# Five chunks of up to 128 keys, a block-diagonal P, a 64-byte pad tile, and low weight words read as unsigned integers

## The chip, the cores and the metric

One core of one Trainium2 chip runs the whole program. The metric is the device time of one execution in microseconds, the median of three executions. One more execution was recorded by the hardware profiler; all rows below come from it.

## The reference, cut to what matters

Three parts run one after another: an attention in two steps, a dense layer, and a layer of eight experts of which each token takes two.

```python
# batch 8, heads 8, seq 576, head_dim 64, 32 rows in p
p_packed = sm_attn(p, k, v)            # 32 query rows against 576 keys
out = sm_attn(q, p_packed, p_packed)   # 576 query rows against the 32 packed rows
x = out as (4608, 512)
h = x @ w_in; g = h - tanh(h); x = g @ w_out      # w_in, w_out are 64-bit floats
...                                               # gate, top 2 of 8 experts, their two matmuls
```

`sm_attn` is softmax attention: scores times 1/8, minus the row's largest, exponential, divided by the row's sum, times the values. The weights `w_in` and `w_out` arrive as 64-bit floating-point numbers, which the kernel turns into 32-bit ones itself.

## The kernel before, in words

The change lies in the first phase (`phase_a`, line 108 of the profile's numbering and on) and in the class `Widen` (line 48 on). The phases after it are the dense layer with the second attention step (`phase_b`, its steps of `g1`, `gate`, `gsplit` and `g2`), and the experts (`PhaseC`).

**Phase A** does the first attention step, `p_packed`, for 16 groups of four heads, and beside it converts weights. It runs 18 steps, n = 0 to 17. Step n computes the scores of group n (`s1`, L175), their largest (`max1`, L180 and L181) and the exponential (`exp1`, L187). For group n-1 it transposes the exponentials on the tensor engine (`t1`, L199), copies them from PSUM to SBUF on ScalarE (`a1t`, L204), multiplies with the values (`pv`, L211), scales and masks on VectorE (`pz2`, L216), transposes (`pt`, L221), copies (`pt_out`, L226) and stores (`pt_store`, L230).

*Scores.* A tile of kT holds 128 partitions: for each of two pairs j of heads, the 64 components of head 0 in partitions 0 to 63 and those of head 1 in partitions 64 to 127, 576 keys and 32 columns of P each. Four matmuls per half c of the keys take 64 rows and 32 columns of the array each and write the 32 rows of their head.

*Values.* The 576 keys are cut in six chunks of 96. So there are six transposes, one copy of 96 x 768, and six times two matmuls of 96 rows and 64 columns, which add up in PSUM. The tile v has 96 partitions of 6 x 256 values, filled by one DMA.

*Weights.* Each step n below 14 also converts two chunks of 128 x 512 weights, c0 = 2n and c1 = 2n+1 (16 of `w_in`, 12 of `w_out`; four more follow in phase B). A chunk arrives as pairs of 32-bit words. `act1` (L69, ScalarE) takes the absolute value of the high word read as a float. `dve` (VectorE) clamps it (L73), shifts it into a 32-bit exponent and mantissa (L75), adds the sign (L76), builds from the low word a float between 1 and 2 by a shift and an or (L78), and cuts the exponent out (L80). `act2` (L84, ScalarE) turns L78's result into the small fraction that the low word stands for. `dve2` (VectorE) multiplies it by the exponent (L88) and adds both parts (L91).

*Order.* The tensor engine, ScalarE and SyncE (which issues the DMAs) work in the order written out by hand in `ORDER` (L103); VectorE's order in this phase is not written by hand. Per step ScalarE runs: `a1t` of n-1, `act1` of c0 (p0), `act2` of c0 (p2), `exp1`, `act1` of c1 (r0), `pt_out` of n-1, `act2` of c1 (r2). The tensor engine runs `t1` of n-1, `s1` of n, `pv` and `pt` of n-1. SyncE issues kT of n+2 (L160), a weight chunk (L144), the store of n-1 (L230), v of n+1 (L166), a weight chunk. There are two buffers of kT and of v, three of the raw weights. In steps 3 to 8 the first piece of the second attention step is put in between (L299 to L335).

**Phase B** starts with the last four chunks of `w_out` converted the same way, in an order written by hand on VectorE too.

**The pool of the experts' small tables** (`consts`, L1101) lies in SBUF above the tiles that were placed after it: among them the 32-bit weights `WI`, the ring `wt`, the first slot of first-layer expert weights and the experts' inputs.

Of the kernel before, what the change touches and what calls it, by code (L numbers as in the profile page):

```python
# [10 lines left out]
F32 = mybir.dt.float32  # L11
FR = mybir.dt.float32r
I32 = mybir.dt.int32
BF = mybir.dt.bfloat16
AF = mybir.ActivationFunctionType
ALU = mybir.AluOpType
# [5 lines left out]
P = 128  # L22
NB, NH, S, D = 8, 8, 576, 64
# [27 lines left out]
class Widen:  # L51
# [19 lines left out]
    def dve(self):  # L71
        V, c = self.K.nc.vector, self.c
        V.tensor_scalar(c, c, EXP_LO, EXP_HI, op0=ALU.max, op1=ALU.min)  # L73
        self.a = a = self.tile("a", I32)
        V.tensor_scalar(a, c.bitcast(I32), 3, 0x3FFFFFFF, op0=ALU.logical_shift_left, op1=ALU.bitwise_and)  # L75
        V.scalar_tensor_tensor(a, self.hi, _sint(0xC0000000), a, op0=ALU.bitwise_and, op1=ALU.bitwise_or)  # L76
        self.f = self.tile("f", I32)
        V.tensor_scalar(self.f, self.lo, 9, 0x3F800000, op0=ALU.logical_shift_right, op1=ALU.bitwise_or)  # L78
        self.t = self.tile("t", I32)
        V.tensor_scalar(self.t, a, _sint(0xFF800000), None, op0=ALU.bitwise_and)  # L80

    def act2(self):
        u = self.f.bitcast(F32)
        self.K.nc.scalar.activation(u, u, AF.Copy, scale=2.0 ** -20, bias=-(2.0 ** -20))  # L84

    def dve2(self):
        G, u = self.K.nc.vector, self.f.bitcast(F32)
        G.tensor_tensor(u, u, self.t.bitcast(F32), op=ALU.mult)  # L88
        if self.w is None:
            self.w = self.t.bitcast(F32)  # L90
        G.tensor_tensor(self.w, u, self.a.bitcast(F32), op=ALU.add)  # L91
# [12 lines left out]
ORDER = """t1 a1t s1 p0 lk p1 max1 p2 p4 pl r4 rec pv pz2 p3 exp1 pt r0 pto pts qs r1 lv qm qx r2 r3 qa rl""".split()  # L104
ENG = {mybir.EngineType.PE, mybir.EngineType.SP, mybir.EngineType.Activation}
NWA = 12


def phase_a(K, kT, v, w_in, w_out, wide_in, wide_out):
    nc, tc = K.nc, K.tc  # L110
    V, A, SY, PE = nc.vector, nc.scalar, nc.sync, nc.tensor
    K.wof = [None] * 16
    CW = 512
    with ExitStack() as ctx:
# [16 lines left out]
        TT, CV = [{} for _ in range(16)], {}  # L131
# [24 lines left out]
        def load_k(n):  # L156
            b, G = BG[n]
            t = TT[n]
            kp = ld.tile([P, 2, S + 32], F32, tag="kT", name=f"kT{n}")
            SY.dma_start(kp, kT[b, G].rearrange("p (j n) -> p j n", j=2))  # L160
            t["k"], t["p"] = kp[:, :, :S], kp[:, :, S:]

        def load_v(n):
            b, G = BG[n]
            TT[n]["v"] = ld.tile([96, 6, 4 * D], F32, tag="v", name=f"v{n}")
            SY.dma_start(TT[n]["v"], v[b, G].rearrange("p (c n) -> p c n", c=6))  # L166

        def s1(n):
            t = TT[n]
            t["s1"] = psb.tile([P, 2, 512], F32, tag="big", name=f"s1_{n}")  # L170
            for c in range(2):
                for h in range(4):
                    j, r = divmod(h, 2)
                    r = slice(64 * r, 64 * r + 64)
                    PE.matmul(t["s1"][32 * h:32 * h + 32, c, :288], t["p"][r, j, :], t["k"][r, j, c * 288:(c + 1) * 288], start=True, stop=True)  # L175

        def max1(n):
            t = TT[n]
# [16 lines left out]
        def t1(n):  # L195
            t = TT[n]
            t["tp"] = psb.tile([P, 8, P], F32, tag="big", name=f"tp{n}")
            for i in range(6):
                PE.transpose(t["tp"][:96, i, :], t["a1"][:, i * 96:(i + 1) * 96], K.ident)  # L199

        def a1t(n):
            t = TT[n]
            t["a1T"] = wk.tile([96, 6, P], F32, tag="a1T", name=f"a1T_{n}")
            A.activation(t["a1T"], t.pop("tp")[:96, :6, :], AF.Copy)  # L204

        def pv(n):
            t = TT[n]
            t["pv"] = ps.tile([P, 512], F32, tag="ps", name=f"pv{n}")
            for i in range(6):
                for j in range(2):  # L210
                    PE.matmul(t["pv"][64 * j:64 * j + 64, :P], t["a1T"][:, i, 64 * j:64 * j + 64], t["v"][:, i, P * j:P * j + P], start=(i == 0), stop=(i == 5))  # L211

        def pz2(n):
            t = TT[n]
# [645 lines left out]
class PhaseC:  # L860
# [240 lines left out]
    def consts(self):  # L1101
        K, V, mp, G = self.K, self.K.nc.vector, self.mp, self.K.nc.gpsimd
        K.sel = mp.tile([P, 4, 4, 32], F32, name="sel")
        for b in range(4):
            for q in range(4):
                G.tensor_copy(K.sel[:, b, q], K.ident[:, 32 * b:32 * b + 32])

        def halves(p, n, pat, cm, name):
            f, i, j = mp.tile([p, n], F32, name=f"half{name}"), mp.tile([p, n], I32, tag=f"t0{name}", name=f"hi{name}"), mp.tile([p, n], I32, tag=f"t1{name}", name=f"hj{name}")
            o = mp.tile([p, n], F32, name=f"odd{name}")  # L1110
            G.iota(f, pattern=pat, base=0, channel_multiplier=cm, allow_small_or_imprecise_dtypes=True)
            V.tensor_copy(i, f)
            V.tensor_scalar(j, i, 1, None, op0=ALU.bitwise_and)
            V.tensor_scalar(i, i, 1, None, op0=ALU.logical_shift_right)
            V.tensor_copy(f, i)
            V.tensor_copy(o, j)
            even, place = mp.tile([p, n], F32, name=f"even{name}"), mp.tile([p, n], F32, name=f"place{name}")
            V.scalar_tensor_tensor(place, f, 2.0, o, op0=ALU.mult, op1=ALU.add)
            V.tensor_scalar(even, o, 2.0, -1.0, op0=ALU.mult, op1=ALU.add)
            V.tensor_tensor(f, f, even, op=ALU.mult)  # L1120
            V.tensor_scalar(even, o, -1.0, 1.0, op0=ALU.mult, op1=ALU.add)
            return f, even, place

        K.need = mp.tile([P, NE], F32, name="need")
        G.iota(K.need, pattern=[[1, NE]], base=1 - NEARLY, channel_multiplier=0, allow_small_or_imprecise_dtypes=True)
        V.tensor_scalar(K.need, K.need, 128.0, None, op0=ALU.mult)
        V.memset(K.need[:, :NEARLY], -1e6)
        K.last = mp.tile([P, E], F32, name="last")
        V.tensor_scalar(K.last, K.eio, float(E - 1), None, op0=ALU.is_equal)
        K.early = mp.tile([NE, 3], F32, name="early")  # L1130
        G.iota(K.early[:, 0:1], pattern=[[0, 1]], base=0, channel_multiplier=1, allow_small_or_imprecise_dtypes=True)
        K.needc = mp.tile([NE, 1], F32, name="needc")
        V.tensor_scalar(K.needc, K.early[:, 0:1], 128.0, 128.0 * (1 - NEARLY), op0=ALU.mult, op1=ALU.add)
        V.tensor_scalar(K.early[:, 1:2], K.early[:, 0:1], 36.0 * (E - 1) - NEARLY, None, op0=ALU.add)
        V.tensor_scalar(K.early[:, 2:3], K.early[:, 0:1], float(NEARLY), None, op0=ALU.is_ge)
        V.scalar_tensor_tensor(K.early[:, 0:1], K.early[:, 2:3], float(-NEARLY), K.early[:, 0:1], op0=ALU.mult, op1=ALU.add)

        self.planr = halves(1, NM, [[1, NM]], 0, "r")
        self.planc = halves(NM, 1, [[0, 1]], 1, "c")
# [276 lines left out]
def layout(inputs):  # L1416
    import numpy as np
    c = np.ascontiguousarray
    x = {k: np.asarray(v) for k, v in inputs.items()}
    wide = {k: x[k].dtype.itemsize == 8 for k in ("moe_w_in", "moe_w_out")}  # L1420

    def words(t):
        return t.view(np.int64) if t.dtype.itemsize == 8 else t

    def heads(t):
        t = t.reshape(NB, 2, 2, 2, S, D).transpose(0, 1, 3, 5, 2, 4)
        return c(t).reshape(NB, 2, P, 2 * S)

    pt = x["p"].reshape(NB, 2, 2, 2, 32, D).transpose(0, 1, 3, 5, 2, 4)
    a = {  # L1430
        "qT": heads(x["q"]),
        "kT": np.concatenate([heads(x["k"]).reshape(NB, 2, P, 2, S), pt.reshape(NB, 2, P, 2, 32)], -1).reshape(NB, 2, P, 2 * (S + 32)),
        "v": c(x["v"].reshape(NB, 2, 4, 6, 96, D).transpose(0, 1, 4, 3, 2, 5)).reshape(NB, 2, 96, 6 * 256),
        "w_in": words(c(x["moe_w_in"].reshape(4, P, FF).transpose(1, 0, 2))).reshape(P, 4 * FF),
        "w_out": words(c(x["moe_w_out"].reshape(16, P, DM).transpose(1, 0, 2))).reshape(P, 16 * DM),
        "w_gate": c(x["moe2_w_gate"]),
        "w_noise": c(x["moe2_w_noise"]),
        "noise": c(x["moe2_noise"].reshape(NB, 6, 96, E).transpose(0, 2, 1, 3)).reshape(NB, 96, 6 * E),
        "w1": c(x["moe2_w1"].reshape(E, 4, P, 2, 512).transpose(0, 2, 3, 1, 4)).reshape(E, P, 4 * F2),
        "w2": c(x["moe2_w2"].reshape(E, 4, 8, 32, DM).transpose(0, 1, 3, 2, 4)).reshape(E, P, 8 * DM),  # L1440
    }
    return a, wide
# [17 lines left out]
```

## Time and profile before

| what | value |
|---|---|
| three executions: median, lowest, highest | 1700.99, 1699.13, 1701.72 us |
| the profiled execution: time, span of its instructions | 1702.0, 1700.3 us |
| TensorE, VectorE, ScalarE, GpSimd busy | 95%, 66%, 51%, 34% of the span |
| mean granted TensorE clock | 0.968 of full speed |
| moved by DMA | 293.62 MB, mean 173 GB/s |

The profiled execution took 1702.0 us, 1.0 us above the median of the three. Its span, 1700.3 us, is the time from the first instruction to the last; 1.7 us lie around it. Engines are PE (tensor engine's matmuls), PEld (its weight loads), DVE (VectorE), ACT (ScalarE), POOL (GpSimd) and SP (SyncE). In brackets a row says how long the engine was idle before the instruction and what ended that.

### The profile page before, as it was taken

The page shows a single profiled execution, that of the slowest core. Times are in us where ns is not written, and L with a number is a line of the kernel's source. Part 1 is how long each engine was busy: PE and PEld are TensorE (multiplying, and loading weights), DVE is VectorE, ACT ScalarE, POOL GpSimd, SP SyncE. Part 2 cuts the span into 40 slices and gives each one's busy share as a digit, 9 for nine tenths or more (in the row PEclk, how much of TensorE's full clock was granted, in tenths as well). Part 3 has the DMA queues.
Part 4 walks back from the last instruction along what each step waited for, and adds up shares of the span by engine and source line. Part 5 has one row for each costly group of instructions (what it writes and reads, how often), then busy time and mean ns, then how long its engine had stood idle before and what let it go on. Part 6 is the DMA issues. An engine that isn't in the chain of part 4 may idle for free.

```text
span 1700.3 us, 29332 instructions
## 1 busy us (share of the span) xinstructions
PE 1617.0 (95%) x10031; PEld 1372.1 (81%) x10031; DVE 1127.2 (66%) x2900; ACT 873.9 (51%) x1848; POOL 569.9 (34%) x560
## 2 busy tenths in 40 slices
PE   5667999999999999999999999999999999999996
PEld 3334889898989898989977788888888888888885
DVE  7886867676767677876665476666666566666652
ACT  3444555555555555543457665555555555555552
POOL 0000200021212121131555475554444455544421
PEclk7677999999999999999999999999999999999998
DMA  8784267676777777753188346452543624554262
GB/s 277 230 269 142 72 216 238 219 227 217 229 235 240 242 236 244 228 181 115 36 247 261 117 111 208 143 149 51 160 133 100 196 50 143 149 167 128 49 208 46
DMA packets 145655, 293.62 MB, mean 173 GB/s; under 512 B 19679, under 2 KB 69130, under 8 KB 140380
## 3 DMA queue, kind: packets, MB, share of 16 engines
q1 hardware_dynamic: 121676, 252.17, 44.5%
q0 software_dynamic: 23824, 39.51, 12.8%
q8 instruction: 81, 1.33, 0.3%
q14 instruction: 74, 0.61, 0.1%
HBM read 670.57 MB, written 107.59 MB: 458 GB/s over the span
## 4 chain that ended last, share of the span: by engine, by line
PE 84%; DVE 7%; ACT 4%; DMA 2%; issue 1%; POOL 1%; POOLq 0%; DVEq 0%; ACTq 0%
PE acc L503 23%; PE py L1214 21%; PE ph L1173 21%; PE h L478 12%; ACT ht L1195 2%; PE u L444 2%; PE s L175 1%; PE tp L199 1%; PE pv L211 1%; PE sq L299 1%; PE lg L524 1%; DVE cva L76 0%; DMA kT<-in_kT_dram 0%; DVE hl L1204 0%; DMA cvr<-in_w_out_dram 0%
## 5 line engine op out<-in xcount | busy, mean ns | idle before, releaser
L1195 ACT ACTIVATE ht<-h 32x256 f32<-32x256 f32 x660 | 274.7, 416 | 229.8 <-DVE h L1175 209.9
L1006 POOL DMA_INDIRECT x<-x1d,gidxm x264 | 254.9, 966 | 277.1 <-DVE xt L1016 203.2
L503 PE MATMUL acc<-gh,wol 128*128 128x288 f32 x1024 | 302.2, 295 | 0.3 <-POOL wol L101 0.3
L1173 PE MATMUL ph<-w0s,xh 128*128 128x512 f32 x1200 | 301.8, 393 | 0.0
L503 PE MATMUL acc<-gh,woh 128*128 128x288 f32 x1024 | 301.6, 295 | 0.0
L503 PE MATMUL acc<-gl,woh 128*128 128x288 f32 x1024 | 301.4, 294 | 0.0
L1214 PE MATMUL py<-w1s,hh 128*128 128x512 f32 x1200 | 286.8, 391 | 3.4 <-ACT hh L1199 1.8
L1175 DVE STREAM_TRANSPOSE h<-ph 128x512 f32<-128x512 f32 x150 | 107.3, 715 | 246.6 <-PE ph L1173 240.2
L1214 PEld LDWEIGHTS py<-w1s,hh 128*128 128x128 f32 x1200 | 224.6, 188 | 54.6 <-ACT hh L1199 4.7
L1173 PEld LDWEIGHTS ph<-w0s,xh 128*128 128x128 f32 x1200 | 225.1, 188 | 50.8 <-issue 0.5
L659 POOL DMA_INDIRECT table<-d,qi x96 | 97.3, 1013 | 309.9 <-DVE g L487 207.8
L503 PEld LDWEIGHTS acc<-gh,wol 128*128 128x128 f32 x1024 | 192.6, 188 | 0.6 <-POOL wol L101 0.6
L503 PEld LDWEIGHTS acc<-gh,woh 128*128 128x128 f32 x1024 | 193.0, 189 | 0.0
L503 PEld LDWEIGHTS acc<-gl,woh 128*128 128x128 f32 x1024 | 192.7, 188 | 0.0
L485 ACT ACTIVATE t<-h 128x288 f32<-128x288 f32 x256 | 104.4, 408 | 146.4 <-PE h L478 145.9
L1193 DVE TENSOR_SCALAR ht<-h 32x256 f32<-32x256 f32 x540 | 166.5, 308 | 9.9
L478 PE MATMUL h<-a2h,uh 128*128 128x288 f32 x512 | 159.5, 312 | 3.3 <-DVE g L487 2.4
L1173 PE MATMUL ph<-w0s,xl 128*128 128x512 f32 x600 | 162.6, 393 | 0.0
L97 ACT ACTIVATE gh<-g 128x288 fp32r<-128x288 f32 x256 | 113.2, 442 | 87.2 <-DVE g L487 86.2
L487 DVE TENSOR_TENSOR g<-h,t 128x288 f32<-128x288 f32 x256 | 115.7, 452 | 57.0 <-ACT t L485 56.5
L478 PE MATMUL h<-a2h,ul 128*128 128x288 f32 x512 | 151.7, 296 | 0.2 <-DVE ul L453 0.2
L478 PE MATMUL h<-a2l,uh 128*128 128x288 f32 x512 | 151.4, 296 | 0.0
(257 smaller groups left out, 2400.2 us busy)
## 6 DMA issues: line engine op xcount, KB each, us to landing
w0s<-wsp SPq DMA_DIRECT2D x136, 2048.0 KB
w1s<-wsp SPq DMA_DIRECT2D x136, 2048.0 KB
wsp<-wt SPq DMA_DIRECT2D x128, 512.0 KB
wt<-in_w_dram SPq DMA_DIRECT2D x128, 256.0 KB
kT<-in_kT_dram SPq DMA_DIRECT2D x16, 608.0 KB
out_dram<-zero SPq DMA_DIRECT2D x37, 256.0 KB
v<-in_v_dram SPq DMA_DIRECT2D x16, 576.0 KB
q<-in_qT_dram SPq DMA_DIRECT2D x32, 288.0 KB
```

The costliest lines, as they stand in the source:

```text
L97: nc.scalar.activation(hi, src, AF.Copy)
L478: nc.tensor.matmul(h[:, :TN], u[:, G, fs], x[:, G, :], start=(n == 0), stop=(n == 5))
L485: nc.scalar.activation(t, h[:, :TN], AF.Tanh)
L487: PACE[0] = nc.vector.tensor_tensor(g, h[:, :TN], t, op=ALU.subtract).ins
L503: nc.tensor.matmul(ACC[ch][d][:, :TN], w[:, d * P:(d + 1) * P], x, start=(f == 0 and n == 0), stop=(f == 15 and n == 2))
L659: ins = nc.gpsimd.indirect_dma_start(out=K.table, out_offset=IO(ap=qi[:, i:i + 1], axis=0), in_=d[:, i, :], in_offset=None, oob_is_err=True)
L1006: g = K.nc.gpsimd.indirect_dma_start(out=x[:, b, :], out_offset=None, in_=rows, in_offset=IO(ap=gidx[:, c, b:b + 1], axis=0))
L1173: self.tick(K.nc.tensor.matmul(p, xx[:, d * P:(d + 1) * P], w[:, fc, ws, d, :], start=(n == 0), stop=(n == 11)))
L1175: self.last = V.transpose(h[:, 2 * fc:2 * fc + 2].rearrange("p g n -> p (g n)"), p).ins
L1193: V.tensor_scalar(dst, src, 0.0, None, op0=ALU.max)
L1195: K.nc.scalar.activation(dst, src, AF.Relu)
L1214: self.tick(K.nc.tensor.matmul(p, xx[:, f * P:(f + 1) * P], w[:, f // 4, ws, f % 4, :], start=(n == 0), stop=(n == 23)))
```

## The change: what it does

- The keys are cut in five chunks, four of 128 and one of 64: five transposes for six, five times two matmuls for six times two, on up to 128 rows. The copy `a1t` becomes two, 128 x 512 and 64 x 128. The tile v has 128 partitions of 5 x 256 values and is filled by two DMAs, 512 KB and 64 KB (its bytes stay the same).
- P is laid out block-diagonally: 64 columns for each pair of heads, zero where a head's rows meet the other head's columns. So `s1` takes two matmuls of 128 rows and 64 columns per half c for four of 64 rows and 32 columns. The tile kT grows from 608 to 640 values per partition and pair, from 608 KB to 640 KB.
- `Widen` loses L78. `act2` reads the low words as unsigned integers straight from the raw chunk, times 2 to the power -52, and writes the tile f.
- A tile `pad` of 16 values (64 bytes per partition), which nothing reads or writes, is put into the pool of the experts' tables.

```diff
     def dve(self):
...
-        self.f = self.tile("f", I32)
-        V.tensor_scalar(self.f, self.lo, 9, 0x3F800000, op0=ALU.logical_shift_right, op1=ALU.bitwise_or)
+        self.f = self.tile("f", F32)
...
     def act2(self):
-        u = self.f.bitcast(F32)
-        self.K.nc.scalar.activation(u, u, AF.Copy, scale=2.0 ** -20, bias=-(2.0 ** -20))
+        self.K.nc.scalar.activation(self.f, self.lo.bitcast(U32), AF.Copy, scale=2.0 ** -52)
...
+NK = 5
+KL = S - P * (NK - 1)
+KC = [(i, min(P, S - P * i)) for i in range(NK)]
...
-            kp = ld.tile([P, 2, S + 32], F32, tag="kT", name=f"kT{n}")
+            kp = ld.tile([P, 2, S + 64], F32, tag="kT", name=f"kT{n}")
...
-            TT[n]["v"] = ld.tile([96, 6, 4 * D], F32, tag="v", name=f"v{n}")
-            SY.dma_start(TT[n]["v"], v[b, G].rearrange("p (c n) -> p c n", c=6))
+            TT[n]["v"] = t = ld.tile([P, NK, 4 * D], F32, tag="v", name=f"v{n}")
+            vv = v[b, G].rearrange("p (c n) -> p c n", c=NK)
+            SY.dma_start(t[:, :NK - 1], vv[:, :NK - 1])
+            SY.dma_start(t[:KL, NK - 1], vv[:KL, NK - 1])
...
             for c in range(2):
-                for h in range(4):
-                    j, r = divmod(h, 2)
-                    r = slice(64 * r, 64 * r + 64)
-                    PE.matmul(t["s1"][32 * h:32 * h + 32, c, :288], t["p"][r, j, :], t["k"][r, j, c * 288:(c + 1) * 288], start=True, stop=True)
+                for j in range(2):
+                    PE.matmul(t["s1"][64 * j:64 * j + 64, c, :288], t["p"][:, j, :], t["k"][:, j, c * 288:(c + 1) * 288], start=True, stop=True)
...
-            for i in range(6):
-                PE.transpose(t["tp"][:96, i, :], t["a1"][:, i * 96:(i + 1) * 96], K.ident)
+            for i, m in KC:
+                PE.transpose(t["tp"][:m, i, :], t["a1"][:, i * P:i * P + m], K.ident)
...
-            t["a1T"] = wk.tile([96, 6, P], F32, tag="a1T", name=f"a1T_{n}")
-            A.activation(t["a1T"], t.pop("tp")[:96, :6, :], AF.Copy)
+            t["a1T"] = wk.tile([P, NK, P], F32, tag="a1T", name=f"a1T_{n}")
+            tp = t.pop("tp")
+            A.activation(t["a1T"][:, :NK - 1], tp[:, :NK - 1], AF.Copy)
+            A.activation(t["a1T"][:KL, NK - 1], tp[:KL, NK - 1], AF.Copy)
...
-            for i in range(6):
+            for i, m in KC:
                 for j in range(2):
-                    PE.matmul(t["pv"][64 * j:64 * j + 64, :P], t["a1T"][:, i, 64 * j:64 * j + 64], t["v"][:, i, P * j:P * j + P], start=(i == 0), stop=(i == 5))
+                    PE.matmul(t["pv"][64 * j:64 * j + 64, :P], t["a1T"][:m, i, 64 * j:64 * j + 64], t["v"][:m, i, P * j:P * j + P], start=(i == 0), stop=(i == NK - 1))
...
+        mp.tile([P, 16], F32, name="pad")
```

The host's layout of k, p and v follows these tiles (P with its zeros, v padded to 640 keys in memory).

## Rows read from the trace of the kernel before

**Rows 1.** Busy time by stretch: PE, PEld, DVE, ACT, POOL, then granted clock, DMA share, GB/s.
```profile
12.42:30.45 18.03, 12.18 (x94) 7.44 (x94) 14.45 (x35) 6.97 (x14) 0.00 (x0) 0.75 0.91 288
30.45:84.59 54.14, 32.19 (x253) 19.87 (x255) 46.15 (x107) 22.59 (x44) 2.68 (x2) 0.63 0.73 232
84.59:127.12 42.53, 27.59 (x237) 16.57 (x239) 38.05 (x95) 20.85 (x40) 0.00 (x0) 0.70 0.81 271
127.12:143.32 16.20, 12.09 (x96) 7.57 (x98) 12.00 (x31) 6.11 (x12) 0.00 (x0) 0.61 0.80 236
...
210.00:1700.30 1490.30, 1471.22 (x8887) 1272.02 (x8887) 959.60 (x2511) 777.58 (x1653) 549.39 (x515) 1.00 0.57 169
```

**Rows 2.** Timeline of step 4 and its follower: start, duration, instruction.
```profile
38.86 2.15 PE L175 MATMUL s<-kT 64*32 64x288 f32 x16
...
40.30 0.54 SPq L166 DMA_DIRECT2D v<-in_v_dram  x1
...
41.07 0.76 DVE L180 TENSOR_REDUCE nm<-s 128x1 f32<-128x576 f32 x1 [1.70 <-PE s L175]
...
42.68 0.42 DVE L78 TENSOR_SCALAR cvf<-cvr 128x512 int32<-128x512 int32 x1
...
43.13 0.63 ACT L84 ACTIVATE cvf<-cvf 128x512 f32<-128x512 f32 x1 [5.12 <-DVE cvf L78]
...
43.67 0.79 ACT L204 ACTIVATE a1T<-tp 96x768 f32<-96x768 f32 x1
...
44.51 2.83 PE L211 MATMUL pv<-v,a1T 96*64 96x128 f32 x24 [3.51 <-ACT a1T L204]
...
46.33 0.72 ACT L187 ACTIVATE a<-s,nm 128x576 f32<-128x576 f32 x1
```

**Rows 3.** Who waited for whom, 30.45 to 84.59: total, times, longest.
```profile
ACT cvf L84 <- DVE cvf L78: 28.8, 9, 6.3
...
PE pv L211 <- ACT a1T L204: 10.5, 4, 3.5
DVE nm L180 <- PE s L175: 7.7, 5, 1.7
```

**Rows 4.** The same view, 84.59 to 127.12.
```profile
PE pt L221 <- DVE Pz L216: 13.9, 5, 4.7
...
DVE nm L180 <- PE s L175: 3.1, 2, 1.7
```

**Rows 5.** Groups by line and shape, 84.59 to 127.12: count, busy, mean ns.
```profile
L199 PE MATMUL tp<-ident,a 128*96 128x128 f32 x30 | 7.4, 416 | 1.1 <-ACT a L187 1.1
...
L84 ACT ACTIVATE cvf<-cvf 128x512 f32<-128x512 f32 x10 | 6.3, 631 | 6.9 <-DVE cvf L78 6.8
...
L69 ACT ACTIVATE cvc<-cvr 128x512 f32<-128x512 f32 x9 | 6.0, 665 | 0.7 <-DMA cvr<-in_w_out_dram 0.7
...
L78 DVE TENSOR_SCALAR cvf<-cvr 128x512 int32<-128x512 int32 x10 | 4.2, 417 | 0.0
...
L204 ACT ACTIVATE a1T<-tp 96x768 f32<-96x768 f32 x5 | 4.0, 803 | 1.2 <-PE tp L199 1.2
...
L226 ACT ACTIVATE PT<-pt 128x128 f32<-128x128 f32 x5 | 1.3, 269 | 0.6 <-ACT cvc L69 0.6
```

**Rows 6.** VectorE's timeline: an L78 in a busy stretch, and the next instruction.
```profile
94.69 0.42 DVE L78 TENSOR_SCALAR cvf<-cvr 128x512 int32<-128x512 int32 x1
95.02 0.42 DVE L80 TENSOR_SCALAR cvt<-cva 128x512 int32<-128x512 int32 x1
```

**Rows 7.** Busy time in a stretch in which the DMA engines are full.
```profile
110.00:115.00 5.00, 2.09 (x32) 1.29 (x24) 4.29 (x9) 0.90 (x2) 0.00 (x0) 0.84 1.01 336
```

**Rows 8.** Timeline of VectorE and of ScalarE at the last chunk, in phase B.
```profile
201.77 0.42 DVE L78 TENSOR_SCALAR cvf_b<-wor 128x512 int32<-128x512 int32 x1
...
202.23 0.63 ACT L84 ACTIVATE cvf_b<-cvf_b 128x512 f32<-128x512 f32 x1 [2.88 <-DVE cvf_b L78]
```

**Rows 9.** The page's costliest groups: one of phase B's matmuls.
```profile
L503 PE MATMUL acc<-gh,wol 128*128 128x288 f32 x1024 | 302.2, 295 | 0.3 <-POOL wol L101 0.3
```

More of the change, by code (lines that the diff above doesn't have):

```diff
@@ L13 @@
 I32 = mybir.dt.int32
+U32 = mybir.dt.uint32
 BF = mybir.dt.bfloat16
@@ L82, in act2 @@
     def act2(self):
-        u = self.f.bitcast(F32)
-        self.K.nc.scalar.activation(u, u, AF.Copy, scale=2.0 ** -20, bias=-(2.0 ** -20))
+        self.K.nc.scalar.activation(self.f, self.lo.bitcast(U32), AF.Copy, scale=2.0 ** -52)
     def dve2(self):
-        G, u = self.K.nc.vector, self.f.bitcast(F32)
+        G, u = self.K.nc.vector, self.f
         G.tensor_tensor(u, u, self.t.bitcast(F32), op=ALU.mult)
@@ L1427, in heads @@
         return c(t).reshape(NB, 2, P, 2 * S)
-    pt = x["p"].reshape(NB, 2, 2, 2, 32, D).transpose(0, 1, 3, 5, 2, 4)
+    p = x["p"].reshape(NB, 2, 2, 2, 32, D).transpose(0, 1, 3, 5, 2, 4)
+    pt = np.zeros((NB, 2, 2, D, 2, 2, 32), p.dtype)
+    for r in range(2):
+        pt[:, :, r, :, :, r] = p[:, :, r]
+    vp = np.zeros((NB, 2, 4, NK * P, D), x["v"].dtype)
+    vp[:, :, :, :S] = x["v"].reshape(NB, 2, 4, S, D)
     a = {
         "qT": heads(x["q"]),
-        "kT": np.concatenate([heads(x["k"]).reshape(NB, 2, P, 2, S), pt.reshape(NB, 2, P, 2, 32)], -1).reshape(NB, 2, P, 2 * (S + 32)),
-        "v": c(x["v"].reshape(NB, 2, 4, 6, 96, D).transpose(0, 1, 4, 3, 2, 5)).reshape(NB, 2, 96, 6 * 256),
+        "kT": np.concatenate([heads(x["k"]).reshape(NB, 2, P, 2, S), pt.reshape(NB, 2, P, 2, 64)], -1).reshape(NB, 2, P, 2 * (S + 64)),
+        "v": c(vp.reshape(NB, 2, 4, NK, P, D).transpose(0, 1, 4, 3, 2, 5)).reshape(NB, 2, P, NK * 256),
         "w_in": words(c(x["moe_w_in"].reshape(4, P, FF).transpose(1, 0, 2))).reshape(P, 4 * FF),
```

## The prediction

> **What bounds the kernel now.** First the busy time by stretch [rows 1]. From 210 us to the end the tensor engine is busy for 1471.22 of 1490.30 us at full clock, and the change adds and removes no instruction there. So what the first 210 us give up, the whole gives up. The four stretches above it are cut where the scores `s1` of steps 1, 3, 8, 13 and 15 are done; they hold 2, 5, 5 and 2 steps of 9.0, 10.8, 8.5 and 8.1 us. The tensor engine is busy for 65% or less of the two middle ones, at clocks of 0.63 and 0.70. VectorE is busy for 46.15 of 54.14 us and for 38.05 of 42.53 us. The DMA engines are at 0.91 in the first stretch, 0.73 and 0.81 in the next two.
>
> Then one step in order of time [rows 2]. The transposes of group 3 are done when `s1` starts at 38.86. Yet their copy L204 runs at 43.67, because ScalarE works in order and stands before L84 (the `act2` of the chunk before) for 5.12 us, until VectorE has run L78 at 42.68. So `pv` starts at 44.51, after 3.51 us of idle tensor engine, and `exp1` (L187) comes at 46.33, long after the reduction at 41.07. VectorE in turn idles 1.70 us for the scores. Over the five steps of this stretch [rows 3] ScalarE waits 28.8 us for L78, `pv` 10.5 us for the copy and VectorE 7.7 us for scores. In the five steps after it [rows 4] the loop is another one: the tensor engine waits 13.9 us for VectorE's Pz, and VectorE only 3.1 us for scores. There VectorE's own work is the pace.
>
> **The change part by part.** *L78 goes.* A mean instruction takes 0.417 us [rows 5], but in a busy stretch the next one starts 0.33 us after it [rows 6], so 0.33 us is what VectorE gets back: 28 x 0.33 = 9.2 us in phase A, 4 x 0.33 = 1.3 us in phase B.
>
> *The wait of `act2` goes.* It needs only the raw chunk now, which `act1` before it has read already. So the copy L204 follows the transposes, during `s1`, and `pv` follows `s1`. Late next in these steps is VectorE's work.
>
> *`act2` reads words with a step of two, as integers.* No row has ScalarE read integers. Below, 631 ns as now [rows 5]; the nearest row is L69, which reads the other word of each pair with the same step, 665 ns [rows 5]; above, I allow twice that. I take 665: 28 x 0.03 = 1 us of ScalarE, which is busy for 20.85 of 42.53 us [rows 1]; cost 0. Without that cover it is 1 us, at the upper end 28 x 0.7 = 19 us of ScalarE's time, still inside its idle share. The raw buffer is now held until `act2`; the load that waits for it needs the chunk three before, which ScalarE has passed by then: 0.
>
> *`pv` and `t1`.* Twelve matmuls take 2.83 us [rows 2], so ten take 2.36: 0.47 us less at the lower clock. Six transposes take 7.4 / 5 = 1.48 us [rows 5], five 1.23. Together 0.7 us a step on an engine that waits: nothing in steps 2 to 13, but on the chain in the last two, which have no weights beside them: I take 1.0 us there.
>
> *`s1`.* Eight matmuls of 288 columns run four beside each other, 2.15 us [rows 2]. Four matmuls would take the same if they run in pairs, and about twice that one by one. `pv` already runs pairs of 64 columns on the same rows: 0.236 us for a pair of 128 columns, which for 288 gives 0.53 us, and four of those (two halves of keys, two records a matmul) are 2.1 us. I take 0; up to 2 us a step otherwise, most of it in the tensor engine's 2.8 us of wait a step [rows 4].
>
> *`a1t` in two.* 631 + 269 ns (L84's shape, L226's) against 803 [rows 5]: 0.1 us more on ScalarE. It may also gain, as `pv` could start after the first piece: 0, bounds -0.1 and +0.2 us a step.
>
> *v in two DMAs, kT larger.* SyncE issues one more DMA a step, 0.54 us by the row of L166 [rows 2]. Behind it stands one weight chunk, which is read a step later: 0; at most 0.5 us a step without that cover. Per step 2.36 MB move for 2.33. At the 336 GB/s of a full stretch [rows 7] a step needs 7.0 us, 0.1 more. I take 0.2 us in all, at the start, where the first kT is waited for. The Trainium skill (SBUF — State Buffer, "Door 1: The DMA port swizzle") speaks against the split: it asks for 128 partitions and one DMA, since 64 partitions reach half of the ports. By its 196 GB/s for 64 partitions, an estimate, the 64 KB would cost 0.14 us more a step, 2 us in all if the transfers set the pace; no run here shows it, and the sum goes without it.
>
> *The pad* moves the tiles placed after it by 64 bytes. The four buffers of gh in phase B lie 1,152 bytes apart, so at different places within 256 bytes, and their matmuls still take 295 ns in the mean [rows 9]: 0. One per cent of the last stretch would be 15 us either way; I see no sign of it.
>
> **The sum.** VectorE's remaining work plus the idle time that the third stretch shows, 42.53 - 38.05 = 4.5 us in five steps. Second stretch: 46.15 - 3.3 + 4.5 = 47.3 for 54.14, 6.8 us less. Third: 38.05 - 3.3 + 4.5 = 39.2 for 42.53, 3.3 less. The first has its transfers at 0.91: 0.6 less. The last: 1.0 less from VectorE, and 1.0 from the shorter tensor work after the weights are through. Phase B: 1.3 less; ScalarE's 2.88 us wait for L78 there [rows 8] mostly hides under VectorE's queue. With 0.2 for the start: 0.6 + 6.8 + 3.3 + 1.0 + 1.0 + 1.3 - 0.2 = 13.8 us. The profiled 1702.0 becomes 1688.2; the median of the runs stands 1.0 us lower: **1687.2 us**.
>
> **The rivals.** *All waits fall away.* Nothing but VectorE's work and the 7.0 us of transfers a step is left: the second stretch 42.8, the third 35.1, the first 15.6, the last 14.0 us. That is 11.3 + 7.4 + 2.4 + 2.2 less, with 1.0 + 1.3 behind them 25.6 us: 1675.4. For it: the tensor engine has more than 2 us a step to spare [rows 4]. Against: engines working in order never meet so well, and 0.91 for 18 us is the fullest stretch now.
>
> *Transfers set the pace.* If the DMA engines can't be kept fuller than in the third stretch (271 GB/s), a step takes 8.7 us: the third stretch loses 1.0, the first and the last gain nothing, the second still gains 6.8. 6.8 - 1.0 + 1.0 + 1.3 - 0.2 = 7.9 less: 1693.1. For it: two or three buffers a kind, and a store in SyncE's queue that waits for the step's end.
>
> *The time is hidden anyway.* ScalarE stands elsewhere for as long, for a raw chunk or for the reduction before `exp1`, and VectorE waits in place of L78; only 1.0 + 1.3 us are left: 1698.7. Against: the copy L204 has nothing else to wait for in rows 2.
>
> *Slower: VectorE's new order.* Its queue in phase A is not written by hand, and an instruction less may put the reduction of the scores behind weights. The loop from `s1` over reduction, exponential and transposes back to `s1` is 2.15 + 0.9 + 0.9 + 1.2 = 5.2 us. A chunk without L78 is about 2.8 us of VectorE. The loop passes today's 9.4 us a step from 4.2 us of delay on, one and a half chunks; with two it is 10.8, times 13 steps is 18 us more: 1719. Against: the reduction now starts where the scores end, with VectorE waiting for it [rows 2].
>
> **How the numbers follow.** The forecast has 0.52 (1682 to 1692), transfers 0.17, all waits gone 0.16, hidden 0.08, slower 0.07 with what else could go wrong, the pad among it. A measurement of this kernel can tell about 0.2%, 3.4 us, from no change. So faster is 0.52 + 0.17 + 0.16 = 0.85, the same 0.08, slower 0.07. The range leaves out the hidden and the slower case: 1675 to 1697.
>
> **What would show it.** Right: no wait of L84 for VectorE; `pv` starts within 0.3 us of the end of `s1` in steps 2 to 5; five steps from 30 us on take some 47 us, the next five 39; 210 us becomes some 196; the long stretch is unchanged. Wrong: ScalarE's waits move to raw chunks with the DMA share near 0.9 (transfers); L180 starts late after `s1` (order); `s1` takes 4 us (no pairs); a longer last stretch (the pad).

## The result, and the profile after

The changed kernel takes 1680.3 us (median of 4 runs, 1678.18 to 1682.72) where the kernel before takes 1700.06 us (4 runs, 1698.93 to 1701.72): 19.8 us less, a ratio of 0.9887 with a 95% interval of 0.9872 to 0.9902. The profiled execution took 1678.18 us; its span is 1676.5 us. It is the fastest of its four, and the profiled execution of before (1702.0 us) is slower than all four of its runs, so the two profiles lie 23.8 us apart.

Where the time went is read first from one mark, the copies `xr<-acc` that close the dense layer's blocks: the first of 64 starts when phase A and the start of phase B are through, the last when the experts' main stage begins. In the kernel before (that tile's instructions: count, least, median and largest duration, first and last start):

```profile
L511 ACT ACTIVATE xr<-acc x64: 402/412/434, 210.4 to 853.3; 128x288 f32<-128x288 f32 x64
```

and in the changed one:

```profile
L515 ACT ACTIVATE xr<-acc x64: 402/412/433, 194.1 to 837.5; 128x288 f32<-128x288 f32 x64
```

The first copy comes 16.3 us earlier, the last 15.8 us, and the end (1700.3 against 1676.5) 23.8 us. So the dense layer gives nothing, and 8.0 us come from the experts' stage, in which no instruction was changed. Such a mark moves by some 3 us between executions of the same work (210.4 us here, 207.2 us in the pad's own run below). There the page's costliest groups show one difference, in the first matmuls of the experts. Before:

```profile
L1173 PE MATMUL ph<-w0s,xh 128*128 128x512 f32 x1200 | 301.8, 393 | 0.0
...
L1173 PE MATMUL ph<-w0s,xl 128*128 128x512 f32 x600 | 162.6, 393 | 0.0
```

and after, 389 ns each for 393, and 7.1 us less busy time in the two groups together:

```profile
L1178 PE MATMUL ph<-w0s,xh 128*128 128x512 f32 x1200 | 296.9, 389 | 0.0
...
L1178 PE MATMUL ph<-w0s,xl 128*128 128x512 f32 x600 | 160.4, 389 | 0.0
```

The stretches after, cut where the scores of the same steps are done (columns as in [rows 1]); the last row runs from the first `xr` copy to the end:

```profile
12.26:25.77 13.51, 9.33 (x68) 5.68 (x64) 12.33 (x28) 6.51 (x14) 0.00 (x0) 0.75 0.97 351
25.77:69.56 43.79, 26.66 (x187) 15.54 (x186) 39.91 (x94) 20.05 (x46) 2.94 (x2) 0.69 0.87 293
69.56:112.59 43.03, 27.24 (x171) 15.68 (x170) 39.73 (x91) 20.87 (x47) 0.00 (x0) 0.66 0.80 265
112.59:128.48 15.89, 11.09 (x73) 6.93 (x74) 12.28 (x29) 7.36 (x19) 0.00 (x0) 0.62 0.75 236
194.10:1676.50 1482.40, 1462.96 (x8887) 1271.24 (x8885) 962.80 (x2511) 776.97 (x1653) 550.27 (x515) 1.00 0.58 170
```

Against [rows 1] the first stretch loses 4.5 us, the second 10.4; the third gains 0.5. The second and third have to be taken together, because the pieces of the second attention step slid from one into the other: 96.7 us became 86.8, or 8.7 us a step.

Who waited for whom, 25.77 to 69.56 (engine, line, releaser: total, times, longest):

```profile
ACT cvc L70 <- DMA cvr<-in_w_in_dram: 17.6, 8, 5.3
...
PE pv L215 <- ACT a1T L207: 8.4, 4, 3.5
```

and from 69.56 to 112.59:

```profile
ACT cvc L70 <- DMA cvr<-in_w_out_dram: 16.2, 7, 4.2
...
PE pv L215 <- ACT a1T L207: 8.9, 4, 3.2
...
PE pt L225 <- DVE Pz L220: 5.2, 5, 2.8
DVE nm L182 <- PE s L177: 1.1, 1, 1.1
```

The 28.8 us that ScalarE stood before `act2` [rows 3] are gone, and the tensor engine's wait for Pz fell from 13.9 us [rows 4] to 5.2. In their place ScalarE stands 33.8 us before `act1` (L70 now), for raw weight chunks to land, and what is behind it in ScalarE's order, the copies of the transposes (L207), comes late for `pv` again: 17.3 us. One turn of the new loop in the timeline:

```profile
89.13 1.50 SPq L146 DMA_DIRECT2D cvr<-in_w_out_dram  x1
...
93.29 2.19 PE L177 MATMUL s<-kT 128*64 128x288 f32 x8
...
95.41 0.66 ACT L70 ACTIVATE cvc<-cvr 128x512 f32<-128x512 f32 x1 [3.43 <-DMA cvr<-in_w_out_dram]
...
95.97 0.26 ACT L230 ACTIVATE PT<-pt 128x128 f32<-128x128 f32 x1
96.13 0.66 ACT L83 ACTIVATE cvf<-cvr 128x512 f32<-128x512 uint32 x1
...
96.26 0.33 SPq L234 DMA_DIRECT2D ptd<-PT  x1
96.68 0.38 SPq L169 DMA_DIRECT2D v<-in_v_dram  x1
96.69 0.59 ACT L207 ACTIVATE a1T<-tp 128x512 f32<-128x512 f32 x1
...
97.33 1.55 PE L215 MATMUL pv<-v,a1T 128*64 128x128 f32 x12 [1.85 <-ACT a1T L207]
97.68 0.54 SPq L146 DMA_DIRECT2D cvr<-in_w_out_dram  x1
```

ScalarE idles 3.43 us for a chunk (95.41), then copies PT (95.97); only then can SyncE issue the store of PT (96.26), the two loads of v, and the step's second chunk (97.68), which is 8.55 us after the same issue of the step before (89.13). The chunk that came late is the one that was requested at 89.13, so a late chunk delays the request of a later one. The same wait undoes the forecast's sign that `pv` starts within 0.3 us of the end of `s1` in steps 2 to 5. It holds in step 2; in steps 3 to 5 `pv` comes 1.4, 1.2 and 3.5 us later. Step 5:

```profile
40.97 2.04 PE L177 MATMUL s<-kT 128*64 128x288 f32 x8
...
44.62 0.66 ACT L70 ACTIVATE cvc<-cvr 128x512 f32<-128x512 f32 x1 [5.29 <-DMA cvr<-in_w_in_dram]
...
46.53 2.60 PE L215 MATMUL pv<-v,a1T 128*64 128x128 f32 x20 [3.52 <-ACT a1T L207]
```

Also to be seen in the turn above: the uint32 read with a step of two takes 0.66 us, and eight records of the wide `s1` 2.19 us where sixteen narrow ones took 2.15 [rows 2].

### The profile page after: what moved, and what is told of

Its sections match the earlier page's. It is cut to its first block, busy times and chain, and to the rows that moved or that the text cites. A ratio compares the mean times of both kernels' runs of the same rounds, so it can differ in the third digit from the quotient of the medians.

```text
span 1676.5 us, 28984 instructions
## 1 busy us (share of the span) xinstructions
PE 1598.0 (95%) x9823; PEld 1362.9 (81%) x9823; DVE 1122.8 (67%) x2868; ACT 871.5 (52%) x1864; POOL 571.0 (34%) x560
## 4 chain that ended last, share of the span: by engine, by line
PE 81%; DVE 6%; ACT 5%; DMA 2%; issue 2%; POOL 1%; SPq 0%; POOLq 0%; DVEq 0%; ACTq 0%
PE acc L507 22%; PE py L1219 21%; PE ph L1178 21%; PE h L482 12%; ACT ht L1200 3%; PE u L448 2%; DMA cvr<-in_w_out_dram 1%; PE lg L528 1%; PE sq L303 1%; POOL x L1010 1%; DVE hl L1209 1%; PE pv L215 0%; DVE h L1180 0%; DVE g L491 0%; PE lt L542 0%
## 5 line engine op out<-in xcount | busy, mean ns | idle before, releaser
L1178 PE MATMUL ph<-w0s,xh 128*128 128x512 f32 x1200 | 296.9, 389 | 0.0
```

Of the source, the lines that this page charges most:

```text
L1178: self.tick(K.nc.tensor.matmul(p, xx[:, d * P:(d + 1) * P], w[:, fc, ws, d, :], start=(n == 0), stop=(n == 11)))
```

## The experiments

Each ratio is to the kernel before, measured beside it on the same chip. The first four ran on one chip (before: 1702.37 us), the next four on another (1727.19), three on a third (1728.45) and the last on a fourth (1700.4). The changed kernel was not run beside them: a comparison with it goes through two ratios and is good to some 4 us.

**The pad alone.**

```diff
         K.sel = mp.tile([P, 4, 4, 32], F32, name="sel")
+        mp.tile([P, 16], F32, name="pad")
```

> Kernel before with the 64-byte pad tile alone. Theory A (the pad shortens the experts' first-layer matmuls, whose start-to-start spacing is 231 ns in the kernel before and 226.7 ns in the changed one): the spacing is 226.7 ns here too, 1,800 matmuls give 1,800 x 4.3 ns = 7.7 us, so about 1692.4 us; the first 210 us are unchanged (the first copy of acc to xr stays at 210.4 us). Theory B (the late gain comes with the rest of the change, or differs from run to run): 1700 us and 231 ns.

Measured: 1693.16 us, 9.2 less; ratio 0.9953 (0.9937 to 0.9970). The waits in phase A are those of before (ScalarE 42.0 us for L78, 40.9 before), and the first `xr` copy starts at 207.2 us, 3 us from that of before. From the last copy to the end it takes 841.3 us, and 847 to 850 us in the three kernels that follow, which have no pad. So 64 bytes that nothing reads are worth 8 us (by the ratio) to 9.2 us (by the medians) of the change's 19.8, in the late stage.

**All but the pad.**

```diff
-        mp.tile([P, 16], F32, name="pad")
```

> The changed kernel without the pad tile. Theory A: spacing back at 231 ns, in two values that alternate from block to block, 7.7 us more than the changed kernel: about 1688 us, the first copy of acc to xr stays at 194 us. Theory B: 1680 us.

Measured: 1689.16 us, 13.2 less; ratio 0.9920 (0.9897 to 0.9942). The first copy starts at 194.9 us, as in the changed kernel. 9.2 and 13.2 add up to 22.4 for the 19.8 of both, within the intervals.

**The unsigned reading alone**, in the kernel before:

```diff
-        self.f = self.tile("f", I32)
-        V.tensor_scalar(self.f, self.lo, 9, 0x3F800000, op0=ALU.logical_shift_right, op1=ALU.bitwise_or)
+        self.f = self.tile("f", F32)
...
-        self.K.nc.scalar.activation(u, u, AF.Copy, scale=2.0 ** -20, bias=-(2.0 ** -20))
+        self.K.nc.scalar.activation(self.f, self.lo.bitcast(U32), AF.Copy, scale=2.0 ** -52)
```

> Kernel before with the integer read of the low words alone (L78 gone). Theory C (VectorE's queue and ScalarE's wait for it are what the early part gains from): most of the early 16 us, 12 to 14, so 1686 to 1688 us, no wait of act2 for VectorE. Theory D (the shorter tensor work of five chunks carries half or more of the early gain): at most 8 us, 1692 us or more.

Measured: 1693.42 us, 8.9 less; ratio 0.9950 (0.9934 to 0.9966). That is less than theory C's 12 to 14 us and near theory D's 8; that `act2` no longer waits for VectorE came as C had it. The waits in the first 150 us:

```profile
PE pt L220 <- DVE Pz L215: 39.2, 15, 6.1
ACT cvc L70 <- DMA cvr<-in_w_in_dram: 26.3, 12, 6.4
ACT cvc L70 <- DMA cvr<-in_w_out_dram: 18.9, 11, 3.5
```

By this part alone the wait for L78 has turned into waits for chunks (45.2 us), and the tensor engine's wait for Pz has grown (29.7 us before).

**The five chunks and the wide P alone**: the changed kernel without the pad and with the old L78 and L84.

> Kernel before with five chunks and the block-diagonal P alone (no pad, L78 kept). Theory C: 1 to 3 us less than before, 1697 to 1699 us, because the copy a1T still stands behind act2, which waits for L78. Theory D: 8 us or more less, 1692 us or less.

Measured: 1698.04 us, 4.3 less; ratio 0.9977 (0.9966 to 0.9989). ScalarE's wait for the shift is still there, 18 times and 50.0 us in total. It lies between the two theories (1 to 3 us, 8 or more). 8.9 + 4.3 = 13.2 is the gain of both, so the two edits add up within the intervals (some 2 to 4 us to either side).

**Is VectorE's work what counts?** The changed kernel, in which VectorE still runs the removed shift, into a tile that nothing reads:

```diff
+        self.g = self.pool.tile([P, self.n], I32, tag="cv_g", name=f"cvg_{self.name}", bufs=2) if not self.narrow else None
+        if not self.narrow:
+            V.tensor_scalar(self.g, self.lo, 9, 0x3F800000, op0=ALU.logical_shift_right, op1=ALU.bitwise_or)
```

> The changed kernel, but VectorE still runs the shift-and-or of the old L78 in the first phase, into a tile that nobody reads (28 instructions of about 0.33 us more); act2 still reads the raw words. So VectorE has its old work back while ScalarE's wait for it stays away. Theory E (VectorE's work is the pace of the changed first phase): 28 x 0.33 = 9 us more than the changed kernel, 1688 to 1690 us. Theory F (the landing of the weight chunks, for which ScalarE now waits 47.6 us, is the pace): less than 3 us more, 1680 to 1683 us.

Measured: ratio 0.9888 (0.9871 to 0.9904), that of the changed kernel (0.9887). So the 9 us of theory E are excluded, and theory F's less than 3 us fits. Nothing at all is not shown: two such ratios part some 4 us, and in the profiled execution, the slowest of its four, the last scores come at 132.5 us, 4 later than in the changed kernel. What the shift cost before was in the main the wait of `act2`.

**What the pad does.** Its size was set to 32 bytes, as here, and to 96 (24 values):

```diff
-        mp.tile([P, 16], F32, name="pad")
+        mp.tile([P, 8], F32, name="pad")
```

> The changed kernel with a pad of 32 bytes: the tiles below it start 64 past a multiple of 128 bytes, for 96 without a pad and 32 with 64 bytes. The second slot of first-layer weights lies elsewhere and stays at 32. Theory G (only a start at 96 is slow): 226.7 ns in all blocks as in the changed kernel, 1680 us. Theory H (moving data and weights must stand alike within 64 or 128 bytes): blocks alternate, slower with the slot that stays at 32; 1682 to 1688 us.

> The changed kernel with a pad of 96 bytes: the tiles below it start at a multiple of 128 bytes. Theory G: 226.7 ns in all blocks, 1680 us. Theory H: blocks alternate, slower with the slot that stays at 32. Theory I (a start at a multiple of 64 is the best there is, 32 only better than 96): below 226.7 ns, towards the 213 ns of 512 columns at 2.4 GHz, up to 20 us less.

and, in the kernel before, only the experts' inputs were moved by 64 bytes:

```diff
         self.xp = pool(K, stack, "c_x", 3, side="right")
+        self.xp.tile([P, 16], F32, name="xpad", bufs=1)
```

> Kernel before with 64 bytes of pad between the first slot of first-layer weights and the tiles of the experts' inputs: only the inputs (the moving data) go from 96 to 32, the slot stays at 96, the other slot at 32. If the moving data's start counts alone: 226.7 ns in all blocks, 1692 us. If the weights' start counts alone: 228.5 and 233.4 ns in turn as before, 1700 us. If each counts for itself: 226.7 with the slot at 32 and some 231 ns with the one at 96, about 1696 us.

In these matmuls the inputs are the operand that stands in the array, 128 x 128 at a time, and 512 columns of the experts' weights move through it; the expectations, which call the inputs the moving data, have the two the wrong way round. The experts' first-layer weights alternate between two tiles, from block to block of 24 matmuls. The first lies among the tiles that the pad moves, the second does not. The table gives the byte, modulo 128, at which the inputs `xh` and `xl` and the two weight tiles start in the built kernels, and the mean time from one start of a matmul to the next in the trace, over the 32 or 33 blocks of the long stretch on each tile:

| kernel | inputs | first weights | second weights | ns on the first | ns on the second |
|---|---|---|---|---|---|
| before | 96 | 96 | 32 | 228.5 | 233.4 |
| changed (also pad alone) | 32 | 32 | 32 | 226.7 | 226.7 |
| inputs alone moved | 32 | 96 | 32 | 229.6 | 226.7 |
| pad of 32 bytes | 64 | 64 | 32 | 227.8 | 233.1 |
| pad of 96 bytes | 0 | 0 | 32 | 227.7 | 233.3 |

The same in the timeline of the tensor engine. Before, a block on the first and one on the second tile, each up to the `py` that follows:

```profile
1009.83 2.01 PE L1173 MATMUL ph<-w0s,xh 128*128 128x512 f32 x8
...
1012.59 1.98 PE L1173 MATMUL ph<-w0s,xh 128*128 128x512 f32 x8
...
1015.31 3.80 PE L1214 MATMUL py<-w1s,hh 128*128 128x512 f32 x16
...
1020.76 2.03 PE L1173 MATMUL ph<-w0s,xh 128*128 128x512 f32 x8
...
1026.36 3.82 PE L1214 MATMUL py<-w1s,hh 128*128 128x512 f32 x16
```

5.48 and 5.60 us for 24 matmuls. With only the inputs moved:

```profile
1016.53 2.01 PE L1174 MATMUL ph<-w0s,xh 128*128 128x512 f32 x8
...
1022.04 3.84 PE L1215 MATMUL py<-w1s,hh 128*128 128x512 f32 x16
...
1027.53 1.98 PE L1174 MATMUL ph<-w0s,xh 128*128 128x512 f32 x8
...
1032.97 3.33 PE L1215 MATMUL py<-w1s,hh 128*128 128x512 f32 x14
```

5.51 and 5.44 us: now the first tile is the slow one and the second the fast one, with neither weight tile moved. So it is not the place of the inputs alone or of the weights alone that counts. The third expectation, that each counts for itself, has nearly these two values; but by it inputs and weights both at 96 would be the slowest pair of all, and they take 228.5 ns. What fits all five kernels is whether both start at the same byte modulo 128. A smaller modulus does not fit, as 32 and 96 are alike modulo 64; a larger one does, since the pairs that are alike here are so modulo 512 too.

This is no rule for every matmul. The dense layer's matmuls of 288 columns, `acc<-gh,wol`, start every 132.0 ns in the kernel before where `gh` starts at 96 and the weights at 32, and every 133.6 ns where both start at 96.

In the rows of before the two halves of the first block also differ (2.76 and 2.72 us), although inputs and weights start alike there. The pads of 32 and 96 bytes show the same; blocks with inputs and weights both at 32 do not. Why the beginning of such a block is slower was not tried. The sum fits: (228.5 + 233.4) / 2 - 226.7 = 4.3 ns for each of 1800 matmuls is 7.7 us, for the 8.0 us of the profiles and the 9.2 us of the pad alone. The two odd pads have the time of the kernel without a pad (0.9920): ratios 0.9944 (0.9928 to 0.9961) for 32 bytes and 0.9922 (0.9905 to 0.9938) for 96, beside 0.9888 on the same chip for the kernel with 64 and the shift kept. So theory H's alternation came true and theories G and I did not. The kernel with the inputs alone moved was run once, 1726.86 us for 1727.19 of before; by its spacing it should gain 5 us, which one run can neither show nor exclude.

**Do the chunks set the pace?** The raw chunks loaded three ahead, with four buffers:

```diff
-                raw = cv.tile([P, 2 * CW], I32, tag="cv_raw", name=f"cvr_{i}")
+                raw = cv.tile([P, 2 * CW], I32, tag="cv_raw", name=f"cvr_{i}", bufs=4)
...
         load_v(0)
+        cv_load(2)
...
-                "pl": lambda: cv_load(c0 + 2) if c0 + 2 < 16 + NWA else None, "rl": lambda: cv_load(c1 + 2) if c1 + 2 < 16 + NWA else None,
+                "pl": lambda: cv_load(c0 + 3) if c0 + 3 < 16 + NWA else None, "rl": lambda: cv_load(c1 + 3) if c1 + 3 < 16 + NWA else None,
```

> The changed kernel, with the raw weight chunks loaded three ahead instead of two and four raw buffers in place of three; the computation and its order are the same. Theory L (the landing of chunks is the pace now: a chunk is issued only after the store of the step before, lands some 5 us later, and ScalarE stands before it for 47.6 us of the first 150): the wait of cvc for cvr falls to under 25 us, the last scores are done by about 120 instead of 128.5 us, the first xr copy comes 5 to 12 us earlier, and the ratio to the kernel before is 0.981 to 0.986. Rival B (the DMA engines themselves are full: 0.80 to 0.97 busy, so that an earlier request only queues longer): under 3 us, ratio 0.987 to 0.990, and the wait for cvr stays above 35 us. Rival V (VectorE is the pace, 39.8 of 43 us busy): the wait for cvr falls, pt's wait for Pz takes its place, under 3 us.

and, as an alternative to it, the second chunk issued ahead of the store:

```diff
-... exp1 pt r0 pto pts qs r1 lv qm qx r2 r3 qa rl
+... exp1 pt r0 pto rl pts qs r1 lv qm qx r2 r3 qa
```

> The changed kernel with one place in the order of issue changed: SyncE issues the step's second weight chunk ahead of the store of PT, not behind it and the two loads of v. Buffers and prefetch depth stay. Theory L says that the store is what holds the chunk's request: the request comes 1.5 to 3 us earlier, the wait of cvc for cvr falls by 10 to 25 us, the time by 3 to 8 us: ratio 0.984 to 0.987. Rival B: under 3 us. A rival to both: the chunk then waits for its raw buffer at the head of SyncE's queue, and the store and the loads of v come later: the same or 2 us slower, with a wait of pv for v.

Three ahead: 1702.42 us, ratio 0.9858 (0.9839 to 0.9876). The wait for chunks falls from 47.6 to 8.9 us in the first 150, as expected, but the last scores come at 124.6 us only, the first `xr` copy 3.3 us earlier in place of 5 to 12, and the gain is about 5 us. Ahead of the store: 1697.41 us, ratio 0.9822 (0.9805 to 0.9839), the fastest version, about 11 us better than the changed kernel where 3 to 8 were expected; the wait for chunks falls to 28.1 us. The same stretch of work, from the scores of step 1 to the last ones, 239 instructions of VectorE in each. The changed kernel:

```profile
12.26:128.48 116.22, 74.32 (x496) 43.84 (x494) 104.25 (x239) 54.79 (x124) 2.94 (x2) 0.68 0.84 281
```

and with the chunk issued ahead of the store:

```profile
12.60:118.10 105.50, 68.09 (x496) 43.40 (x494) 99.72 (x239) 56.34 (x124) 2.68 (x2) 0.76 0.88 305
```

10.7 us less, with the DMA engines at 305 GB/s for 281. So it was the request that was late, not the engines that were full. VectorE is now busy for 99.72 of 105.50 us, and the tensor engine's longest wait is for Pz, 35.0 us in the first 150.

**The scores of before**, eight matmuls with narrow P, in the changed kernel:

```diff
-                for j in range(2):
-                    PE.matmul(t["s1"][64 * j:64 * j + 64, c, :288], t["p"][:, j, :], t["k"][:, j, c * 288:(c + 1) * 288], start=True, stop=True)
+                for h in range(4):
+                    j, r = divmod(h, 2)
+                    r = slice(64 * r, 64 * r + 64)
+                    PE.matmul(t["s1"][32 * h:32 * h + 32, c, :288], t["p"][r, j, :], t["k"][r, j, c * 288:(c + 1) * 288], start=True, stop=True)
```

> The changed kernel with the scores of before: eight matmuls with 32 columns of P each, and the narrow P of before; five chunks, pad and unsigned reading stay. The prediction priced the wide P at 0, since pairs of matmuls run beside each other: ratio within 0.002 of the changed kernel's (0.987 to 0.991), and s1 takes 2.15 us at the low clock in both. Rival: the pairs cost up to 1 us a step on the chain and the eight narrow ones are worth 3 to 10 us: ratio 0.983 to 0.987. The other rival, that the wide P is worth something by itself (fewer weight loads for the tensor engine): ratio 0.991 to 0.994.

Measured: ratio 0.9881 (0.9865 to 0.9897), the changed kernel's. The wide P shows no gain here, so the 4.3 us of the attention edits are put down to the five chunks and the copy in two pieces; but the comparison is no finer than those 4.3 us, and these parts were not run by themselves.

**Both edits of the loads together.**

> The two edits before taken together: the second weight chunk is issued ahead of the store, chunks are loaded three ahead, with four raw buffers. Theory V2 (with the chunk's request freed from the store VectorE is the pace again: in the variant with the request ahead of the store it is busy for 108.5 of 118.1 us, and pt waits 35.0 us for Pz): no more to gain, the last scores at 116 to 120 us, ratio 0.980 to 0.984. Theory L2 (chunks still set the pace, since SyncE stands 53 us before raw buffers there): the fourth buffer takes that wait away and gives 3 to 6 us more: last scores at 111 to 115 us, ratio 0.977 to 0.980. A rival to both: with the chunks further ahead, kT and v come late, and the time is that of the variant with three ahead alone: ratio 0.985 to 0.988.

Measured: 1686.65 us, ratio 0.9921 (0.9908 to 0.9935): worse than either and than the changed kernel; none of the three theories had that. The same stretch of work:

```profile
12.40:137.20 124.80, 75.81 (x498) 48.28 (x496) 99.99 (x239) 55.58 (x124) 2.68 (x2) 0.70 0.76 258
```

VectorE has the same 100 us of work, in 124.8 us instead of 105.5. Its timeline in a step of this kernel:

```profile
83.81 0.76 DVE L182 TENSOR_REDUCE nm<-s 128x1 f32<-128x576 f32 x1 [1.72 <-PE s L177]
84.48 0.68 DVE L77 SCALAR_TENSOR_TENSOR cva<-cvr,cva 128x512 int32<-128x512 int32 x1
...
87.90 0.42 DVE L80 TENSOR_SCALAR cvt<-cva 128x512 int32<-128x512 int32 x1
88.23 0.14 DVE L183 TENSOR_SCALAR nm<-nm 128x1 f32<-128x1 f32 x1
```

The reduction of the scores is done by 84.6 us, but the 0.14 us that make it the bias of `exp1` (L183) follow only after eight weight instructions, at 88.23, and ScalarE's exponential starts at 88.49, after 4.88 us of idle time, which the profile puts down to the instruction right behind L183. The wait of `exp1` for L183 totals 30.8 us in the first 150, the longest 6.2. With the chunk issued ahead of the store alone, one weight instruction stands between the two:

```profile
78.77 0.75 DVE L182 TENSOR_REDUCE nm<-s 128x1 f32<-128x576 f32 x1
79.44 0.68 DVE L87 TENSOR_TENSOR cvf<-cvf,cvt 128x512 f32<-128x512 f32 x1
80.04 0.14 DVE L183 TENSOR_SCALAR nm<-nm 128x1 f32<-128x1 f32 x1
```

VectorE's order in this phase is not written by hand; it came out regular in one kernel and poor in some steps of the other. Over all 16 steps the time from the start of the reduction to that of L183 adds up to 16.1 us with the chunk ahead of the store and to 35.4 us with both edits, 19.3 us more, and the two stretches differ by 19.3 us. That this order makes the difference is read from the timelines; a kernel with it written out was not run, and what decides it was not tried.

The same sum is 26.5 us before, 19.3 in the changed kernel, 32.5 with the shift kept and 25.3 with the chunks three ahead. So VectorE's order moved in each of these kernels without being meant to. A part of what each edit gave in phase A, up to 7 us of the change's own gain, can be this order; no run parts it from the rest.

## Why the prediction was right, and where it was not

The time, 1680.3 us, lies inside the range, 6.9 us under the forecast of 1687.2. The forecast's own case (1682 to 1692) was passed at its lower end by 1.7 us, through a term that it had at nothing. Without the pad the kernel takes 0.9920 of the time before, some 1686.5 us, which is nearly the forecast; that the pad's gain still fits into the range is luck, since the range was made wide for other reasons.

- *The pad: 0.* This is the step that failed. It measures 9.2 us by the pad alone, and 8.0 us between the profiles. The argument from [rows 9] was that tiles at different places take the same 295 ns. But 1,152 bytes are nine times 128, so those four buffers all start at the same byte modulo 128, and the row could not show it; besides, the 288-column matmuls of that stage show no such difference, and in the experts' stage the time hangs on how both operands start against each other. The other step, "one per cent of the last stretch would be 15 us either way", had the right order of size and was left out of the sum.
- *The rest: 13.8 us.* Without the pad the change measures 13.2 us, and by the first `xr` copy 15.5 us (16.3 in the changed kernel). This is the right size, though not from the stretches named. The two middle ones were to fall from 96.7 to 47.3 + 39.2 = 86.5 us and fell to 86.8; the first lost 4.5 us where 0.6 were forecast, the last and the end of phase A 0.3 for 2.0, and from the last scores to the first `xr` copy 65.6 us were left of 67.1, 1.5 less for the 1.3 of phase B.
- *The wait of `act2` goes.* Right, it is gone, and the unsigned reading alone gives 8.9 us. What was to follow from it did not: the copy still comes late, now behind a chunk, and in the first 150 us `pv` waits 21.6 us for it, 13.7 before. *L78's own 0.33 us on VectorE*, 9.2 us in phase A, was the wrong reason: put back beside the changed kernel it costs at most some 4 us.
- *VectorE's work plus its idle time is the pace.* Wrong as a mechanism: ScalarE waits 47.6 us for chunks in the first 150, the forecast's own sign of the rival. That rival, "transfers set the pace", had 8.7 us a step, which is what the ten middle steps take, and it had named the store in SyncE's queue. But it had the DMA engines unable to be fuller; moving one request ahead of the store brought them from 281 to 305 GB/s and 10.7 us. The sum came out by luck, because both loops are near 8.6 us a step.
- *`pv` and `t1`: 1.0 us.* Undersized: the attention edits alone measure 4.3 us. Whether the shorter matmuls, the copy in two pieces or VectorE's order give it, no run parts.
- *`act2`'s read at 0, `s1` at 0.* Right: 657 ns a read in the mean where 665 was taken, and the narrow scores give the same time within the interval. *The second DMA of v: 0.2.* The Trainium skill (SBUF — State Buffer, "Door 1: The DMA port swizzle") has 196 GB/s for a DMA on 64 partitions, which by the prediction's estimate is 2 us in all for the 64 KB piece of v if transfers set the pace; no run parted v's load from the rest, so this stays open.
- *Slower: VectorE's new order.* Not in this change, where the reduction reaches `exp1` sooner than before (19.3 us in all for 26.5). The last experiment's timelines speak for the danger being real: with the same work that stretch takes 19.3 us more than in the best version, near the price that the rival had named (18).

## What to carry to other kernels

Undo each edit by itself, the ones that look like nothing too: some two fifths of this gain was a tile that nothing reads. Where matmuls run back to back, compare the start-to-start time with that of the same shape elsewhere, and if it is longer, try a start at the same byte modulo 128 for both operands; it helped at 512 columns here and not at 288. When a wait goes, ask what the next one was hiding: a request that stands behind a store in an issuing queue sets a loop of its own, and moving it in the order can be worth as much as the edit. And where an engine's order is left open, look at it again after every edit, since it can move by itself.

## What the runs showed of the hardware

- In the experts' first layer (float32r, 512 moving columns, 128 x 128 standing, granted clock 0.99 in that stage) a matmul starts every 226.7 to 228.5 ns when inputs and weights start at the same byte modulo 128 (32, 96, 64, 0), and every 229.6 to 233.4 ns when they do not (32 against 96, 64 and 0). At 288 columns in the dense layer no such difference shows (132.0 ns for 32 against 96, 133.6 ns for 96 and 96).
- A read of 128 x 512 uint32 words with a step of two by ScalarE takes 657 ns, as the float read of the other words does (673 ns).
- On two of the chips the kernel before takes 25 to 28 us more than on the two others. Profiles from there hold 9 to 15 us of idle tensor engine, mostly in the experts' matmuls, for which they show no releaser; the rest of the difference stays open. The ratios of like kernels agree all the same (0.9888 and 0.9881 there, 0.9887 for the change).
